# Statistics, norms, stores and an opening on TensorE: four edits to an interleaved convolution and FFN kernel

## The chip, the cores and the metric

The kernel runs on one core of a Trainium2 chip, in a single launch. The metric is the time of one execution on the device, in microseconds (us). A smaller number is better.

## What is computed

The reference holds two layers that share their weights. Each adds a gated long convolution and then a GELU-gated FFN to a residual stream x of 2048 tokens by 576 features, which starts as `A_q`. Cut to what matters:

```python
x = x + A(layernorm(x), k, v, shift_k, ssm_k, ssm_D)   # A(q, ...) = q * y
x = x + B(layernorm(x), w_gate, w_up, w_down)
x = x + A(layernorm(x), k, v, shift_k, ssm_k, ssm_D)
x = x + B(layernorm(x), w_gate, w_up, w_down)

kv = (4-tap causal convolution of k with shift_k, per feature) * v
y  = irfft(rfft(kv, padded to 4096) * rfft(ssm_k, padded))[:2048] + kv * ssm_D
B(x) = (gelu_tanh(x @ w_gate) * (x @ w_up)) @ w_down      # 576 -> 4608 -> 576
layernorm(x) = (x - mean) / sqrt(var + 1e-5)              # over the 576 features
```

The inputs and the output are bf16. The convolution's result y depends on k, v and the kernels only, so it is the same in both layers. A gate step is x + (x − mean) · rstd · y, row by row.

## The kernel before

*Tiling.* The tokens are cut into 4 blocks of 512, each of which is 4 tiles of 128 rows (tile j of a block holds every fourth row). The 576 features are handled as two halves of 288 columns. The convolution goes block against block in the frequency domain: the forward transforms, the sums over pairs of blocks and the inverse transforms are matrix products with tables of sines (`G`, `F1`, `F2`), which ScalarE makes at the start. Transformed kernel blocks (`Hd`) and kv blocks (`Kd`) are written to HBM and read back when a later block needs them.

*The FFN* goes in 24 visits. A visit takes one block of one layer (a unit) through one of 3 phases of 12 column tiles: 12 groups of 18 gate and up products (`gu`, L1078), a GELU on ScalarE (L1082), a product on VectorE (L1083), and 96 down products in four tiles j (`dn`, L1093). Units of the same pass share the weights of a phase; the passes are block 0 of layer 0 alone, then pairs, then the last block of layer 1 alone. Weights are loaded by SyncE (SP), into three `wgu` and three `wd` buffers.

*Before visit 0* the order is written out by hand in `begin` (L472 to L673), and each engine works through its own part of that order: the taps of the shift convolution by products of `ones` with the taps (`taps`, L521), the transposes of the first kernel block (L544), the forward products of kernel blocks 0 to 3 (`h_tile`, L563, 16 products by `G`, each half copied by ScalarE at L186), block 0's kv products on VectorE, its forward transforms, products and inverse (`inv0`, L621). Then follow the four gate steps of block 0 (`gate0`), the normalised rows (`norm0`), their transposes by TensorE into `xnT` (`turn0`), and between these the last `h_tile`s and the first products for kv block 1.

*Row statistics* come in two ways. `stat_steps` (L752) takes them on VectorE (`bn_stats` at L759, in two halves, `bn_aggr`, and an add), with the power −0.5 on GpSimd (POOL). `mean_after` (L803) and `square_task` (L810) take the row sum from an operation that accumulates it: POOL makes the negative mean `nm` (L806), ScalarE squares with `nm` as its bias and accumulates (L814), and POOL makes `ve` (L821) and `rstd` (L822). Before, the raw rows of block 0 (`x0_stats`, two calls of two tiles each, L596 and L646) and its gated rows use the first way; all later blocks use the second.

*After the start* a planner emits the other work between the products. It keeps modelled times for TensorE, VectorE and ScalarE and takes the head of a queue when its inputs should be ready: `vq` for residual and norm steps (`prep`, L870; `run_vq`, L917), `aq` for squares, `conv.spills` for what POOL does (spills, stores, `nm`, `rstd`), `conv.V`, `conv.Pq` and `conv.L` for the convolution. A step's place in the program is thereby fixed when the kernel is built. Normalised rows of later blocks are transposed by DMA on SP (`spread`, L903, two transposes per tile). `spreads` issues them, and while a norm is close `weights` (L952) holds back weight loads, which use the same queue. The rows of one tile, from its sum to its transposed rows, are: residual `mul` and `add` (L835, L847), `nm`, square, `rstd`, norm (L874), transposes.

*PSUM* is drawn from two pools: `psp` with 3 buffers, `cpsp` with 1. At the start `ps()` (L108) takes every fourth tile from `cpsp`:

```python
self.nps += 1
if self.startup and self.nps % 4:
    return self.psp.tile([P, 2, 512], F32, tag="pr", name="ps")
return self.cpsp.tile([P, 2, 512], F32, tag="cps", name="cps")
```

*The end.* In the last phase of a layer 1 unit each down tile j is summed with x into an output buffer `ob` (two buffers, L1103), and `conv.store` (L1106, issued at L266) has POOL store it to the output, 16 such stores in all. The program closes at L1164, where every DMA queue is drained.

Of the kernel before, what the change touches and what calls it, by code (L numbers as in the profile page):

```python
# [54 lines left out]
class Conv:  # L55
# [416 lines left out]
    def begin(self, gate0, turn0, x0_stats, more, scratch, wide, stay):  # L472

        tc, nc, D = self.tc, self.nc, self.D
        with ExitStack() as es:
# [44 lines left out]
            jg.append(None)  # L520
            def taps(j):  # L521
                ps = self.ps()
                for h in range(2):
                    nc.tensor.matmul(ps[:, h, 0:HW], lhsT=ones[:], rhs=sk1[:, h * HW:(h + 1) * HW, j], start=True, stop=True)
                nc.scalar.copy(out=self.halves(self.skc[:, j, :]), in_=ps[:, :, 0:HW])
# [70 lines left out]
            x0_stats(0)  # L596
            kc, A = {}, {}
# [48 lines left out]
            x0_stats(1)  # L646
# [3 lines left out]
            more(2)  # L650
            gate0(0)
# [25 lines left out]
def ssm_geglu_kernel(ctx, tc, A_q, A_k, A_v, A_shift_k, A_ssm_k, A_ssm_D, B_x, B_w_gate, B_w_up,  # L677
# [92 lines left out]
    def gate_steps(c, j, v, second):  # L770
        def mul():
            xa = (x_c if second else x_b)[c][:, j, :]
            if second:
                v["t"] = gwork.tile([P, D], F32, tag="g_t", name="g_t")[:]
            else:
                if j == 0:
                    x_c[c] = xpool.tile([P, RT, D], F32, name=f"x_c{c}", tag="x")
                v["t"] = x_c[c][:, j, :]
            nc.vector.scalar_tensor_tensor(out=v["t"], in0=xa, scalar=v["mv"][:, 0:1],
                                           in1=conv.y[c][:, j, :], op0=ALU.subtract, op1=ALU.mult)  # L780
            if second and j == RT - 1:
                conv.y_used[c] = t.dve + 1.0

        def add():
            xa = (x_c if second else x_b)[c][:, j, :]
            nc.vector.scalar_tensor_tensor(out=x_c[c][:, j, :], in0=v["t"], scalar=v["rstd"][:, 0:1], in1=xa,  # L786
                                           op0=ALU.mult, op1=ALU.add)
        return [(("y", c, j), C_ST, mul), (0.0, C_ST, add)]
# [66 lines left out]
    gvars = {}  # L855

# [13 lines left out]
    def prep(ui, j):  # L870
# [46 lines left out]
    def run_vq(limit):  # L917
# [11 lines left out]
        else:  # L929
            r = NEVER if len(xn_made) >= 2 else need[1].get("rstd_at", NEVER)  # L930
# [46 lines left out]
    with tc.manual_schedule():  # L977
        make_identity(nc, ident[:])
        g0 = early_stats(0)
        vs0 = [{} for _ in range(RT)]  # L980
    
        def norm0(j):
            xn = xnp.tile([P, XW], BF16, tag="xn", name="xn")
            v = vs0[j]
            nc.vector.tensor_scalar(out=xn[:, 0:D], in0=x_c[0][:, j, :], scalar1=v["mv"][:, 0:1],
                                    scalar2=v["rstd"][:, 0:1], op0=ALU.subtract, op1=ALU.mult)
# [3 lines left out]
        def turn0(j):  # L990
# [4 lines left out]
            for b in range(NKC):  # L995
                c0 = b * P if b < 5 else HK + (b - 5) * P
                nc.tensor.transpose(pt[:, b // 5, (b % 5) * P:(b % 5 + 1) * P], xn0[j][:, c0:c0 + P], ident[:])
            nc.scalar.copy(out=xnT_of[0][:, 0:5, tok], in_=pt[:, 0, 0:5 * P].rearrange("p (b q) -> p b q", q=P))
            nc.vector.tensor_copy(out=xnT_of[0][:, 5:NKC, tok], in_=pt[:, 1, 0:4 * P].rearrange("p (b q) -> p b q", q=P))
# [169 lines left out]
```

## Time and profile before

| what | us |
|---|---|
| median of 3 runs | 979.71 (978.53 to 980.3) |
| the profiled execution's own time | 979.42 |
| its span in the profile | 977.7 |
| TensorE (PE) busy | 947.3, 97% of the span |
| VectorE (DVE) busy | 542.1, 55% |
| ScalarE (ACT) busy | 301.9, 31% |
| GpSimd (POOL) busy | 139.9, 14% |
| gate and up products, L1078, 5184 of them | 568.8 |
| down products, L1093, 2304 of them | 296.7 |

How to read the profile's lines: a group's line has the line of the code, the engine, the operation, what it writes and reads with the shapes, the count after an x, then the busy time and the mean of one in ns, then the idle time of the engine just before them and what ended most of it. In a view in order of time the first column is the start in us from the span's start, the second the length; a bracket holds the wait before it and what ended that wait. `PEld` is TensorE's weight load, which overlaps its products. SPq and POOLq are the instruction sequences of SP and POOL with their DMA issues. A line such as "x3: 46/108/9861" gives the least, median and longest duration in ns of three such entries, and then the time from the first to the last.

### The profile page before, as it was taken

Reading aid. Unit: us, or ns where it says so; the run is one execution under the profiler, and the core shown is the slowest. Engines: PE = TensorE matmul, PEld = TensorE weight load, DVE = VectorE, ACT = ScalarE, POOL = GpSimd, SP = SyncE. Lnnn points to the kernel's source line nnn. Section 1 sums busy time; section 2 is a strip of 40 time slices with the busy share of each in tenths; the row PEclk is TensorE's granted clock in tenths of the full one; section 3 lists DMA queues with packets and bytes.
Section 4 is the critical chain, followed back from the end, with each engine's and each line's share of the span. In section 5 each row is a group of like instructions: output and inputs, shape, how many; then the busy total and the mean of one; then the engine's idle time right before and its main releaser. Section 6 shows DMA issues by size and latency. Waiting matters only on the chain.

```text
span 977.7 us, 19269 instructions
## 1 busy us (share of the span) xinstructions
PE 947.3 (97%) x8240; PEld 547.4 (56%) x8240; DVE 542.1 (55%) x986; ACT 301.9 (31%) x549; POOL 139.9 (14%) x299
## 2 busy tenths in 40 slices
PE   7979999899999999999999999999999999999995
PEld 4755554536556466465565565466456556556543
DVE  8878887867687476887323333663333335433331
ACT  7845213432222522413212411342211213221120
POOL 2343100521101112412000100130000002100000
PEclk9999999989999999999999999999999999999998
DMA  7989975964952551497360360293540630596710
GB/s 181 309 236 288 263 162 141 203 154 102 234 157 74 113 156 36 92 225 141 71 152 1 72 148 13 50 186 94 99 120 2 126 93 8 108 245 151 146 38 24
DMA packets 128538, 127.48 MB, mean 130 GB/s; under 512 B 45571, under 2 KB 121028, under 8 KB 128452
## 3 DMA queue, kind: packets, MB, share of 16 engines
q1 hardware_dynamic: 119184, 90.26, 43.3%
q0 software_dynamic: 9136, 35.08, 11.2%
q8 instruction: 64, 1.05, 0.5%
q10 hardware_dynamic: 132, 0.91, 0.3%
q14 instruction: 22, 0.18, 0.1%
HBM read 105.58 MB, written 10.62 MB: 119 GB/s over the span
## 4 chain that ended last, share of the span: by engine, by line
PE 80%; issue 13%; DVE 4%; ACT 1%; DMA 1%; POOL 0%; POOLq 0%; SPq 0%; DVEq 0%
PE gu L1078 50%; PE dn L1093 24%; PE cps L232 2%; PE cps L258 1%; PE cps L205 1%; PE ps L184 1%; DMA xnT<-xn 1%; DVE stats L759 0%; POOL out_dram L266 0%; DVE yb L226 0%; DVE prod L222 0%; DVE prod L225 0%; DVE yb L617 0%; DVE kvt L160 0%; DVE x_c L786 0%
## 5 line engine op out<-in xcount | busy, mean ns | idle before, releaser
L1078 PE MATMUL gu<-xnT,wgu 64*128 64x512 bf16 x5184 | 568.8, 377 | 6.7 <-DMA xnT<-xn 3.7
L1078 PEld LDWEIGHTS <-wgu 64*128 64x128 bf16 x5184 | 252.5, 94 | 313.4 <-issue 15.5
L1083 DVE TENSOR_TENSOR hT<-ga,gu 128x512 bf16<-128x512 f32 x288 | 197.9, 687 | 277.3 <-ACT ga L1082 276.2
L1082 ACT ACTIVATE ga<-gu 128x512 f32<-128x512 f32 x288 | 172.0, 597 | 547.4 <-PE gu L1078 546.1
L1093 PE MATMUL dn<-wd,hT 128*128 128x288 bf16 x2304 | 296.7, 286 | 0.0
L1093 PEld LDWEIGHTS <-hT 128*128 128x128 bf16 x2304 | 223.6, 98 | 65.1 <-issue 9.3
L1114 DVE TENSOR_TENSOR x_c<-x_c,dn 128x576 f32<-128x576 f32 x64 | 48.2, 753 | 88.1 <-PE dn L1093 87.8
L806 POOL TENSOR_SCALAR nm<-s 128x1 f32<-128x1 f32 x56 | 18.7, 336 | 372.1 <-DVE x_c L1109 157.8
L814 ACT ACTIVATE junk<-x_c,nm 128x576 bf16<-128x576 f32 x44 | 33.8, 769 | 23.6 <-POOL nm L806 23.6
L266 POOL DMA_DIRECT2D out_dram<-ob x16 | 8.8, 553 | 185.0 <-DVE ob L1103 185.0
L822 POOL TENSOR_TENSOR rstd<-ve,neghalf_t 128x1 f32<-128x1 f32 x56 | 34.6, 617 | 4.7
L226 DVE TENSOR_TENSOR sum<-prod 128x576 bf16<-128x576 bf16 x72 | 33.0, 458 | 3.0
L184 PEld LDWEIGHTS <-G 128*128 128x128 bf16 x256 | 25.6, 101 | 10.6 <-DVE h L546 2.1
L184 PE MATMUL ps<-h,G 128*128 128x288 bf16 x192 | 27.3, 299 | 3.0 <-DVE h L546 1.9
L1103 DVE TENSOR_TENSOR ob<-x_c,dn 128x576 bf16<-128x576 f32 x16 | 12.1, 754 | 31.6 <-PE dn L1093 21.8
L324 POOL DMA_DIRECT2D hr<-Hd x32 | 17.6, 549 | 63.7 <-DVE prod L225 63.5
L316 POOL DMA_DIRECT2D kr<-Kd x24 | 13.4, 560 | 91.6 <-DVE prod L225 91.6
L821 POOL TENSOR_SCALAR ve<-ss 128x1 f32<-128x1 f32 x56 | 16.4, 293 | 60.3 <-ACT junk L814 60.2
L232 PE MATMUL cps<-sum,ident 128*128 128x288 bf16 x144 | 24.9, 287 | 0.0
L160 DVE TENSOR_TENSOR kvt<-k,skc 128x1152 bf16<-128x1152 bf16 x32 | 23.7, 754 | 1.5 <-DMA k<-in_A_k_dram 1.0
L208 ACT COPY eo<-cps 128x576 f32<-128x576 f32 x24 | 15.3, 636 | 15.9 <-PE cps L205 11.1
L213 DVE TENSOR_TENSOR kc<-eo 128x288 bf16<-128x288 f32 x48 | 19.3, 453 | 1.5 <-ACT eo L208 1.5
(111 smaller groups left out, 472.7 us busy)
## 6 DMA issues: line engine op xcount, KB each, us to landing
wgu<-in_B_w_gate_dram SPq DMA_DIRECT2D x45, 576.0 KB, 5.8
wd<-in_B_w_down_dram SPq DMA_DIRECT2D x30, 864.0 KB, 7.0
wgu<-in_B_w_up_dram SPq DMA_DIRECT2D x45, 512.0 KB, 7.8
hr<-Hd POOLq DMA_DIRECT2D x32, 288.0 KB, 4.7
kr<-Kd POOLq DMA_DIRECT2D x24, 288.0 KB, 4.7
Hd<-h POOLq DMA_DIRECT2D x12, 288.0 KB, 4.2
Kd<-kc POOLq DMA_DIRECT2D x12, 288.0 KB, 7.7
k<-in_A_k_dram POOLq DMA_DIRECT2D x3, 1008.0 KB, 11.6
```

What stands on the lines that cost most here:

```text
L160: nc.vector.tensor_tensor(out=st[dst][:], in0=self.kt_[b][:, s0:s0 + 2, :], in1=self.skc[:, j, :].unsqueeze(1).to_broadcast([P, 2, D]), op ...
L184: nc.tensor.matmul(ps[:, h, 0:HW], lhsT=G[:, i, s * NFQ + kt * P: s * NFQ + (kt + 1) * P], rhs=src[:, i, h * HW:(h + 1) * HW], start=(i == ...
L213: self.nc.vector.tensor_tensor(out=dst, in0=eo[:, 0, :], in1=eo[:, 1, :], op=op)
L226: nc.vector.tensor_tensor(out=dst, in0=pr[:, 0, :], in1=pr[:, 1, :], op=ALU.subtract if part == 0 else ALU.add)
L232: nc.tensor.matmul(ps[:, h, 0:HW], lhsT=self.ident[:], rhs=pr[:, h * HW:(h + 1) * HW], start=first, stop=last)
L814: nc.scalar.activation(out=junk[:], in_=get_x(), func=ACT.Square, bias=v["nm"][:, 0:1], accum_out=v["ss"][:])
L822: nc.gpsimd.tensor_tensor(out=v["rstd"][:], in0=ve[:], in1=neghalf_t[:, 0:1], op=ALU.pow)
L1078: nc.tensor.matmul(pair[:, s, :], lhsT=w[r0:r0 + HK, k, gi * P:(gi + 1) * P], rhs=xnT[r0:r0 + HK, b, :], start=(k == 0), stop=(k == NKC - 1))
L1082: nc.scalar.activation(out=ga[:], in_=pair[:, 0, :], func=ACT.Gelu_apprx_tanh)
L1083: nc.vector.tensor_tensor(out=hT[:, fi, :], in0=ga[:], in1=pair[:, 1, :], op=ALU.mult)
L1093: nc.tensor.matmul(acc[:, h, 0:HW], lhsT=hT[:, fi, j * P:(j + 1) * P], rhs=d[:, fi % WT, h * HW:(h + 1) * HW], start=(fi == 0), stop=(fi = ...
L1114: nc.vector.tensor_tensor(out=xh, in0=xh, in1=acc[:, :, 0:HW], op=ALU.add)
```

## The change

Four things are changed.

1. *Block 0's statistics.* The gate's `add` accumulates the row sum, and `mean_after` and `square_task` follow it, in place of `stat_steps` on the gated rows; `gate0` pops `nm`, square and `rstd` from their queues at once. The raw rows of tiles 2 and 3 get their statistics right behind those of tiles 0 and 1. The gate order is 0, 2, 1, 3; `norm0` and `turn0` follow two tiles behind their gates; in the first two turns ScalarE makes both copies to `xnT`. The last `h_tile` stands behind the last turn, and eight instead of four kv products of block 1 are issued before visit 0.
2. *Norms of later blocks.* In layer 0 the norm of a tile is queued two tiles behind its residual step instead of one, and three instead of two normalised tiles may wait for their transposes.
3. *The last visit's stores* are issued by SP, and the last tile is computed half by half, each half with its own output buffer and store.
4. *The opening.* One more PSUM tile is drawn at the start, and 16 products of `ones` with `ones` (128 columns each) write to it. Nothing reads them.

The diff, cut to its core:

```diff
+            ps = self.ps()
+            for _ in range(16):
+                nc.tensor.matmul(ps[:, 0, 0:P], lhsT=ones[:], rhs=ones[:], start=True, stop=True)
+
             def taps(j):
...
             x0_stats(0)
+            x0_stats(1)
             kc, A = {}, {}
...
             pair0(1, 1)
-            x0_stats(1)
             inv0(1)
             inv0(3)
...
+            self.kv1 = self.kv_ops(1)
+            ops = iter(self.kv1)
...
             gate0(0)
+            gate0(2)
             h_tile(2, 2, self.hrp)
-            gate0(2)
             h_tile(2, 1, self.hrp)
+            gate0(1)
+            norm0(0)
             h_tile(2, 3, self.hrp)
-            turn0(0)
-            gate0(1)
+            turn0(0, True)
+            gate0(3)
+            norm0(2)
             h_tile(3, 0, self.hrp)
-            turn0(2)
-            self.kv1 = self.kv_ops(1)
+            turn0(2, True)
+            norm0(1)
+            kv1_ops(2)
+            h_tile(3, 2, self.hrp)
+            norm0(3)
+            turn0(1, False)
+            kv1_ops(2)
             h_tile(3, 1, self.hrp)
-            gate0(3)
-            h_tile(3, 2, self.hrp)
-            turn0(1)
-            for need, op in self.kv1[:2]:
-                op()
+            turn0(3, False)
+            kv1_ops(4)
             h_tile(3, 3, self.hrp)
-            turn0(3)
-            for need, op in self.kv1[2:4]:
-                op()
...
+            v["s"] = small.tile([P, 1], F32, tag="s", name="s")
+            nc.vector.scalar_tensor_tensor(out=x_c[c][:, j, :], in0=x_c[c][:, j, :], scalar=g["rstd"][:, 0:1],
+                                           in1=x_b[c][:, j, :], op0=ALU.mult, op1=ALU.add, accum_out=v["s"][:])
+            mean_after(v, 0.0)
+            square_task(lambda: x_c[c][:, j, :], v)
...
-        if j > 0:
-            tasks.append(norm(j - 1))
+        lag = 2 if layer == 0 else 1
+        if j >= lag:
+            tasks.append(norm(j - lag))
         if j == RT - 1:
-            tasks.append(norm(j))
+            tasks += [norm(i) for i in range(RT - lag, RT)]
...
-            r = NEVER if len(xn_made) >= 2 else need[1].get("rstd_at", NEVER)
+            r = NEVER if len(xn_made) >= 3 else need[1].get("rstd_at", NEVER)
...
+            (nc.scalar.copy if act else nc.vector.tensor_copy)(
+                out=xnT_of[0][:, 5:NKC, tok], in_=pt[:, 1, 0:4 * P].rearrange("p (b q) -> p b q", q=P))
             nc.scalar.copy(out=xnT_of[0][:, 0:5, tok], in_=pt[:, 0, 0:5 * P].rearrange("p (b q) -> p b q", q=P))
-            nc.vector.tensor_copy(out=xnT_of[0][:, 5:NKC, tok], in_=pt[:, 1, 0:4 * P].rearrange("p (b q) -> p b q", q=P))
...
-            for _, _, run in gate_steps(0, j, gvars[0][j], False) + stat_steps(0, j, "l_", vs0[j]):
+            for _, _, run in gate_steps(0, j, gvars[0][j], vs0[j]):
                 run()
-            if seen0:
-                norm0(seen0[-1])
-            seen0.append(j)
-            if len(seen0) == RT:
-                norm0(j)
+            conv.spills.pop()[1]()
+            aq.pop()[2]()
+            conv.spills.pop()[1]()
...
-        conv.step(1, kv=conv.kv1[4:], loaded=True)
+        conv.step(1, kv=conv.kv1[8:], loaded=True)
...
+                if wb == NWB - 1 and j == RT - 1:
+                    dst = out2[c * CH:(c + 1) * CH, :].rearrange("(p j) d -> p j d", j=RT)[:, j, :]
+                    for h in range(2):
+                        for fi in range(FP):
+                            down(fi, h)
+                        ob = work.tile([P, D], BF16, tag="ob", name="ob")
+                        nc.vector.tensor_tensor(out=ob[:, 0:HW], in0=xh[:, h, :], in1=acc[:, h, 0:HW], op=ALU.add)
+                        nc.sync.dma_start(out=dst[:, h * HW:(h + 1) * HW], in_=ob[:, 0:HW])
+                    break
...
-                    conv.store(out2[c * CH:(c + 1) * CH, :].rearrange("(p j) d -> p j d", j=RT)[:, j, :], ob,
-                               t.pe + 0.2 + C_EVD + LAG)
+                    dst = out2[c * CH:(c + 1) * CH, :].rearrange("(p j) d -> p j d", j=RT)[:, j, :]
+                    if wb == NWB - 1:
+                        nc.sync.dma_start(out=dst, in_=ob[:])
+                    else:
+                        conv.store(dst, ob, t.pe + 0.2 + C_EVD + LAG)
```

More of the change, by code (lines that the diff above doesn't have):

```diff
@@ L768, in stat_steps, with gate_steps, early_stats @@
         return [(("xb", c) if pfx == "e_" else 0.0, C_BN, lambda: half(0)), (0.0, C_BN + 0.25, lambda: (half(1), aggr()))]
-    def gate_steps(c, j, v, second):
+    def gate_steps(c, j, g, v):
         def mul():
[L772 to L779, printed above, removed]
+            if c not in x_c:
+                x_c[c] = xpool.tile([P, RT, D], F32, name=f"x_c{c}", tag="x")
+            nc.vector.scalar_tensor_tensor(out=x_c[c][:, j, :], in0=x_b[c][:, j, :], scalar=g["mv"][:, 0:1],
                                            in1=conv.y[c][:, j, :], op0=ALU.subtract, op1=ALU.mult)
-            if second and j == RT - 1:
-                conv.y_used[c] = t.dve + 1.0
         def add():
[L785 to L788, printed above, removed]
+            v["s"] = small.tile([P, 1], F32, tag="s", name="s")
[3 more added lines that the diff above has]
+            square_task(lambda: x_c[c][:, j, :], v)
+        return [(0.0, C_ST, mul), (0.0, C_ST, add)]
+    gvars = {}
+    def early_stats(c):
+        gvars[c] = [{} for _ in range(RT)]
+        return [s for j in range(RT) for s in stat_steps(c, j, "e_", gvars[c][j])]
     aq = deque()
@@ L979, in ssm_geglu_kernel @@
         g0 = early_stats(0)
-        vs0 = [{} for _ in range(RT)]
+        vs0 = [{"pfx": "l_"} for _ in range(RT)]
         def norm0(j):
@@ L1023, in more @@
                 load_x(1)
-        conv.begin(gate0, turn0, lambda k: [run() for _, _, run in g0[4 * k:4 * k + 4]], more,
+        conv.begin(gate0, norm0, turn0, lambda k: [run() for _, _, run in g0[4 * k:4 * k + 4]], more,
                    lambda dt: xtp.tile([P, RT if dt == I32 else 2, D], dt, tag="xnT", name="ang"),
```

26 lines of the change are left out of this document (14 added, 12 removed).

## The prediction

> **What bounds the kernel now.** I read the busy table by stretches first, then the waits of PE, then the order of time at the four places where PE stands. Columns of the first view: stretch, length, busy time and count of PE, weight loads, DVE, ACT, POOL, then clock, DMA share, GB/s.
>
> ```profile
> 42.30:66.10 23.80, 18.30 (x166) 14.30 (x165) 18.97 (x47) 14.74 (x23) 10.00 (x15) 1.00 0.85 231
> 66.10:191.20 125.10, 125.03 (x1066) 70.82 (x1065) 105.63 (x199) 47.09 (x90) 30.53 (x59) 1.00 0.86 219
> 191.20:197.40 6.20, 0.47 (x5) 0.17 (x6) 1.40 (x4) 0.00 (x0) 1.57 (x5) 0.82 0.82 183
> 197.40:966.00 768.60, 768.42 (x6756) 436.56 (x6756) 378.18 (x661) 206.22 (x382) 83.97 (x191) 1.00 0.48 108
> 966.00:977.70 11.70, 0.00 (x0) 0.00 (x0) 0.73 (x1) 0.00 (x0) 0.54 (x1) 0.67 0.04 13
> ```
>
> From 66.1 on PE is full (125.03 of 125.10, 768.42 of 768.60) except at one seam, 191.2 to 197.4, and in the last 11.7 us. The change adds no product there, so only three stretches can give: the front (before 66.1), the seam (at most 6.2 us), the tail (at most 11.7). Of PE's waits in the front the longest in total is (us in total, times, longest):
>
> ```profile
> PE xps L997 <- DVE xn L985: 3.9, 2, 2.7
> ```
>
> PE waits there for block 0's normalised rows, which DVE makes.
>
> **The tail: the last visit's stores on SP, the last one in halves.**
>
> ```profile
> 954.00 11.93 PE L1093 MATMUL dn<-wd,hT 128*128 128x288 bf16 x96
> 965.97 0.76 DVE L1103 TENSOR_TENSOR ob<-x_c,dn 128x576 bf16<-128x576 f32 x1 [2.19 <-PE dn L1093]
> 967.02 0.54 POOL L266 DMA_DIRECT2D out_dram<-ob  x1 [2.40 <-DVE ob L1103]
> DMA to landing us min/median/max: 2.0/2.0/2.0
> L1164 SPq DRAIN  x3: 7/7/7, 969.3 to 977.1; - x3
> L1164 POOLq DRAIN  x3: 46/108/9861, 967.0 to 977.4; - x3
> ```
>
> PE ends at 965.93 (954.00 + 11.93). The store, issued by POOL at 967.02, has landed 2.0 later, at 969.0, and SP drains at 969.3. But POOL's first DRAIN, right behind its last DMA, starts at 967.0 and takes 9.861 us: to 976.9. The program ends 0.8 later, at 977.7. So neither the data nor SP ends the kernel; POOL's drain does, 7.6 us after SP. With the change POOL's last DMA is a store of the visit before (near 864), its drain stands 100 us ahead of the end, and its 9.9 us hide behind the last visit's products.
>
> What is left after PE's end: the wait of DVE (0.04), the half-width sum, SP's pick-up (0.05, an estimate), the landing, SP's 0.3 from landing to drain, and the closing 0.8. For the half sum the row of the same width is
>
> ```profile
> L213 DVE TENSOR_TENSOR kc<-eo 128x288 bf16<-128x288 f32 x48 | 19.3, 453 | 1.5 <-ACT eo L208 1.5
> ```
>
> 0.45. For a landing of an SP store in a quiet chip no row exists; the nearest is POOL's 2.0, the same bytes at the same place, which I take. Sum 0.04 + 0.45 + 0.05 + 2.0 + 0.3 + 0.8 = 3.65 against 977.7 − 965.93 = 11.77: **8.1 off**. Bounds: SP's own DMAs land in 2.5, 3.2 or 9.2 (least, median, most; the row stands with the rivals). With 3.2 the second `ob` buffer comes in too: the last half takes the tile of j = 2, written until 2.14 before PE's end (2.94 per j − 0.04 − 0.76) and free 3.2 + 0.05 later, at +1.1; then 1.1 + 0.45 + 0.05 + 3.2 + 1.1 = 5.9, 5.9 off. Above, nothing is left to gain but the 2.0. I take **8.0, from 5.5 to 8.3**.
>
> The Trainium skill speaks against this: "DMA: Bandwidth & Descriptors", section "Issuing engines are not separate DMA queues", says that the issuing engine only changes the sequencer's issue time. By that alone the move is worth POOL's 0.54 at most; it is the first rival. The same page's table "SWDGE vs HWDGE vs iDMA" gives first bytes at about 0.6 us from SP against 1 us from POOL; by it the sum would be 0.4 better. No run shows either yet.
>
> **The front: row statistics.** Rows of before, in order of time, then groups (busy, mean ns):
>
> ```profile
> 29.18 0.76 DVE L222 TENSOR_TENSOR prod<-kc,h 128x1152 bf16<-128x1152 bf16 x1 [1.69 <-ACT kc L197]
> 42.34 0.81 DVE L759 BATCH_NORM_STATS2 stats<-x_b 128x6 f32<-128x288 bf16 x2
> 44.19 1.14 PE L184 MATMUL ps<-h,G 128*128 128x288 bf16 x8
> 44.78 0.81 DVE L779 SCALAR_TENSOR_TENSOR x_c<-x_b,mv,y 128x576 f32<-128x576 bf16 x1
> 45.05 1.28 ACT L649 ACT_TABLE_LOAD   x1
> 46.46 0.63 ACT L186 ACTIVATE h<-ps 128x576 bf16<-128x576 f32 x1
> 46.55 0.82 DVE L759 BATCH_NORM_STATS2 stats<-x_c 128x6 f32<-128x288 f32 x2
> 57.48 0.98 PE ps L184 x8
> 62.14 0.68 PE L997 MATMUL xps<-ident,xn 128*128 128x128 bf16 x9 [0.74 <-ACT h L186]
> 66.10 17.90 PE L1078 MATMUL gu<-xnT,wgu 64*128 64x512 bf16 x162 [0.82 <-ACT xnT L998]
> L186 ACT ACTIVATE h<-ps 128x576 bf16<-128x576 f32 x10 | 6.4, 649 | 5.3 <-DMA Hd<-h 3.5 <-PE ps L184 1.7
> L998 ACT COPY xnT<-xps 128x640 bf16<-128x640 bf16 x4 | 2.8, 690 | 2.0 <-PE xps L997 2.0
> L806 POOL TENSOR_SCALAR nm<-s 128x1 f32<-128x1 f32 x56 | 18.7, 336 | 372.1 <-DVE x_c L1109 157.8
> L814 ACT ACTIVATE junk<-x_c,nm 128x576 bf16<-128x576 f32 x44 | 33.8, 769 | 23.6 <-POOL nm L806 23.6
> L822 POOL TENSOR_TENSOR rstd<-ve,neghalf_t 128x1 f32<-128x1 f32 x56 | 34.6, 617 | 4.7
> L821 POOL TENSOR_SCALAR ve<-ss 128x1 f32<-128x1 f32 x56 | 16.4, 293 | 60.3 <-ACT junk L814 60.2
> ```
>
> *Moved:* the raw rows' statistics of tiles 2 and 3, 42.34 to 44.78 = 2.44, go ahead of the product at 29.18, where DVE waits 1.69. DVE's work from there on is 2.44 − 1.69 = 0.75 later, and dense, so the first gate product starts at 42.34 + 0.75 = 43.1 instead of 44.78. The inverse products' copies and the table load behind them are 0.75 later too.
>
> *Removed:* four tiles' DVE statistics of x_c, 0.82 for the two halves alone (46.55), so 3.3 and more in all. *Added* per tile: nm 0.34 on POOL, a square 0.77 on ACT, ve 0.29 and rstd 0.62 on POOL, 2.0, and four crossings at 0.1 (an estimate): 2.4 from sum to rstd. The accumulated sum itself costs DVE nothing that I count: under 0.1 per tile.
>
> *The new wait.* ACT and POOL work in order. Tile 0's sum is done at 43.1 + 1.8 = 44.9, nm at 45.3; its square waits for ACT, free after the table load at 46.46 + 0.75 + 0.1 = 47.3, and ends at 48.1; rstd 49.2. Tile 2's sum is done at 46.7, but its nm stands on POOL behind tile 0's rstd: 49.6, its square 49.7 to 50.5. Behind this square on ACT are the copies of h tiles (2,2) and (2,1), which started at 46.46 and now start at 50.5. PE starts these four halves at 44.19 + 0.75 = 44.9, has four PSUM pairs, and stops at 44.9 + 4 × 0.98 = 48.9, until the first is copied at 51.2.
>
> *From 50.5* ACT sets the pace up to the last transposed rows: 12 h copies × 0.65, two squares × 0.77, four xnT copies × 0.69 and the two of four blocks that come over from DVE (0.57 each, an estimate by 0.69 for five): 7.8 + 1.5 + 2.8 + 1.1 = 13.2, with 0.5 for waits: 64.2. PE turns tile 3 just before (62.6 to 63.2, 0.68) and computes the h tile (3,3), now behind that turn, 2 × 0.98: 65.2. Then visit 0 starts; before it did so at 66.5 (162 products × 0.1085 = 17.6, back from 84.0). **1.3 off.** Bounds: a PE without a wait from 44.9, 7 h tiles × 1.96 + 4 × 0.68 = 16.4, starts at 61.3 (5.2 off); if the squares of tiles 1 and 3 also stop ACT, 2.4 − 0.77 = 1.6 each, 1.9 is lost.
>
> *At nothing:* eight instead of four kv products (0.77 each, 3.1 more) before visit 0; they lie on DVE, which has 4.8 idle in this stretch and loses 3.3 of statistics. Uncovered, two of them ahead of tile 3's xnT copy would cost 1.5.
>
> **The opening: 16 dummy products, and one more PSUM tile drawn,** so that every later pool choice shifts by one.
>
> ```profile
> 2.69 1.69 PE L524 MATMUL ps<-sk,ones 1*128 1x288 bf16 x6 [2.69 <-DMA sk<-in_A_shift_k_dram]
> 5.61 2.88 PE L544 MATMUL hps<-ident,hn 128*128 128x128 bf16 x20 [0.72 <-ACT skc L525]
> 10.44 4.95 PE L184 MATMUL ps<-h,G 128*128 128x288 bf16 x24 [1.95 <-DVE h L546]
> 11.40 1.43 DVE L160 TENSOR_TENSOR kvt<-k,skc 128x1152 bf16<-128x1152 bf16 x2 [1.02 <-DMA k<-in_A_k_dram]
> ```
>
> PE is idle to 2.69. Sixteen at the transposes' pace (2.88 / 20 = 0.144) take 2.3 from 1.1: taps 0.7 late, the transposes up to 0.7 late; DVE has 1.02 of wait for k at 11.40 that takes this. If the clock is up sooner, the first 16 h products, some 4.0 long (later ones take 0.98 for eight), save up to 2.0 on PE, but the kv chain on DVE, which waits for k, is next. I take **0, from −0.5 to +0.7**. "TensorE: Matmul & The Clock Gate" of the Trainium skill, section "What's actually happening", wants some 3.4 us of sustained work before full speed and puts a cold 128-column product at 0.107; by it the dummies take 1.7, end as the taps' data come, and cost nothing. Sum unchanged, the +0.7 gone.
>
> **The seam: norms two tiles behind.**
>
> ```profile
> 189.67 0.57 DVE L877 TENSOR_SCALAR xn<-x_c,nm,rstd 128x576 bf16<-128x576 f32 x1
> 186.97 6.03 SPq L906 DMA_TRANSPOSE xnT<-xn  x4
> 197.36 1.89 PE L1078 MATMUL gu<-xnT,wgu 64*128 64x512 bf16 x8 [3.67 <-DMA xnT<-xn]
> ```
>
> In the planned order of after, tile 3's norm follows the third residual sum and two cross sums directly; a product (0.76, as at 29.18) and a sum (some 0.45) that stood between now come later. PE's interleaved forward products put that residual some 0.5 later. So xn, now at 189.67, is 0.7 earlier, its two transposes, and PE's start at 197.36: **0.7 off, from −1 to +4** (the norm of tile 2 moves ahead by 2, and the transposes no longer queue).
>
> **Sum.** 8.0 + 1.3 + 0 + 0.7 = 10.0. The profiled execution took 979.42, 1.7 more than its span of 977.7, and the median of the runs is 979.71: 979.4 − 10.0 = 969.4, and 969.7 by the median. I say 969.6.
>
> **Rivals.**
> 1. *The drain stays* (does not do what it says): the 9.9 us are a closing routine of POOL that waits for all engines, wherever its last DMA was. For it: all queues close with a DRAIN. Against: POOL's starts at 967.0, before SP and the landing, with no wait before it. Then 979.7 − 2.0 − 0.5 = 977.2. Chance 0.10.
> 2. *ACT becomes the bound of the front* with POOL's order in it, and the seam gives nothing: lost 1.9 there, 979.7 − 8.0 + 1.9 = 973.6. For it: ACT's 13.2 from 50.5 leave it no slack. Against: PE has 1.96 per tile to do meanwhile. Chance 0.10.
> 3. *Slower: the transposes of the last block queue behind a weight load.*
>
> ```profile
> 648.09 23.42 PE gu L1078 x216
> 632.38 0.64 SPq L733 DMA_DIRECT2D wgu<-in_B_w_gate_dram  x1
> L906 SPq DMA_TRANSPOSE xnT<-xn x40: 1199/1252/2227, 211.4 to 671.0; - x40
> DMA to landing us min/median/max: 2.5/3.2/9.2
> ```
>
> In after's SP order three weight loads stand ahead of all eight transposes of block 3; before, four went first. They start at 632.4 + 2.0 = 634.4; PE needs them at 648.1, with the next pass. At the median of 1.25 to issue and 3.2 they are there at 634.4 + 7 × 1.25 + 3.2 = 646.4. It decides from 1.5 each; at the largest values of the row, 634.4 + 7 × 2.23 + 9.2 = 659.2, PE stands 11.1: 969.6 + 11.1 = 980.7. Chance 0.04.
>
> Forecast 0.76, its own range 967.0 to 972.5. The range of all: 966.5 to 974.0, which takes in rival 2 and the bounds of tail and front. Within 0.2% (2.0 us, what a measurement can tell) lies half of rival 1, so faster 0.91, same 0.05, slower 0.04.
>
> **What would show it.** Tail: POOL's long DRAIN ends long before the last product; from PE's last product to the end 3.5 to 6 us. Front: first gu product near 65.2; a wait of the ACT square on POOL's nm near 48 to 50; PE standing near 49 to 51. Seam: PE's wait for xnT about 0.7 shorter. Wrong: a POOL DRAIN of 10 us that ends with the kernel, or a new wait of PE between 200 and 960.

## The result and the profile after

The changed kernel takes 974.18 us (median of 5 runs, 973.51 to 976.38); the kernel before took 979.47 beside it (5 runs, 978.53 to 980.3). The ratio is 0.9952, interval 0.9937 to 0.9967: faster by some 5, where 10 were forecast, and 0.2 above the range of 966.5 to 974.0. The profiled execution took 973.51 with a span of 971.7, which is 6.0 less than the 977.7 of before.

The busy table of the changed kernel, cut where PE starts visit 0, where it stops and starts at the seam, and where its last product ends (columns as in the prediction):

```profile
42.30:65.82 23.52, 19.43 (x174) 15.08 (x172) 15.28 (x31) 18.15 (x33) 10.74 (x20) 1.00 0.84 225
65.82:191.57 125.75, 125.34 (x1067) 69.47 (x1066) 100.83 (x191) 47.76 (x91) 29.56 (x60) 1.00 0.86 213
191.57:199.46 7.89, 0.01 (x1) 0.00 (x1) 0.81 (x3) 0.00 (x0) 1.29 (x4) 0.80 1.15 271
199.46:968.36 768.90, 768.32 (x6758) 436.70 (x6758) 381.41 (x666) 206.22 (x382) 83.09 (x188) 1.00 0.48 108
968.36:971.70 3.34, 0.00 (x0) 0.00 (x0) 0.45 (x1) 0.00 (x0) 0.00 (x0) 0.92 0.08 25
```

The tail shrank from 11.77 to 3.34, but PE's last product ends at 968.36, 2.4 later than before (965.93). PE's waits say where (us in total, times, longest):

```profile
PE gu L1087 <- DMA xnT<-xn: 7.9, 1, 7.9
PE dn L1103 <- DVE ob L1112: 0.5, 1, 0.5
PE cps L205 <- ACT eo L208: 0.3, 1, 0.3
```

At the seam (where PE goes from the last down product of visit 2 to the first gate product of block 1) PE now stands 7.9 in one piece. Before it was 3.7 for these rows and 2.1 just ahead of that, which the profile puts down to a step of DVE: 5.8 in all. The 0.5 is new and stands in the halved last tile.

**Tail.** The last visit in order of time, and the drains (least/median/longest in ns, first and last start):

```profile
966.22 0.45 DVE L1112 TENSOR_TENSOR ob<-x_c,dn 128x288 bf16<-128x288 f32 x1 [0.72 <-PE dn L1103]
966.73 1.63 PE L1103 MATMUL dn<-wd,hT 128*128 128x288 bf16 x12 [0.55 <-DVE ob L1112]
968.39 0.45 DVE L1112 TENSOR_TENSOR ob<-x_c,dn 128x288 bf16<-128x288 f32 x1 [1.72 <-PE dn L1103]
L1187 POOLq DRAIN  x3: 46/107/12017, 865.8 to 971.5; - x3
L1187 SPq DRAIN  x3: 7/7/7, 970.9 to 971.2; - x3
```

POOL's long drain (12.0 now) starts at 865.8 and is over 90 us ahead of the end. The bracket in the second row is the price of the halves: the second half's first product waits until DVE has read the first half.

**Front,** in order of time:

```profile
43.23 0.81 DVE L786 SCALAR_TENSOR_TENSOR x_c<-x_b,mv,y 128x576 f32<-128x576 bf16 x1
49.36 0.78 ACT L827 ACTIVATE junk<-x_c,nm 128x576 bf16<-128x576 f32 x1 [1.16 <-POOL nm L819]
50.81 1.14 PE L184 MATMUL cps<-h,G 128*128 128x288 bf16 x8 [1.65 <-ACT h L186]
63.26 0.66 PE L1009 MATMUL xps<-ident,xn 128*128 128x128 bf16 x9
65.82 6.43 PE L1087 MATMUL gu<-xnT,wgu 64*128 64x512 bf16 x58
```

These are the forecast's own steps: gate at 43.1, ACT's square behind POOL's nm, PE standing from 48.9 to about 51, tile 3's turn by 63.2, first gate product at 65.2. In the first row the gate starts at 43.23; the brackets of the second and third are ACT's wait for `nm` and PE's standing, from 49.16 to 50.81.

**Seam.** SP, DVE, POOL and PE in order of time, then the seam's later transposes (ns to issue, first and last start) with their landing, of the changed kernel:

```profile
180.78 0.62 SPq L745 DMA_DIRECT2D wgu<-in_B_w_gate_dram  x1
183.19 11.48 SPq L918 DMA_TRANSPOSE xnT<-xn  x6
189.36 0.57 DVE L888 TENSOR_SCALAR xn<-x_c,nm,rstd 128x576 bf16<-128x576 f32 x1
189.47 0.62 POOL L760 DMA_DIRECT2D x_b<-in_A_q_dram  x1
190.81 1.07 POOL L263 DMA_DIRECT2D Kd<-kc  x2 [0.72 <-DVE kc L213]
199.49 2.82 PE L1087 MATMUL gu<-xnT,wgu 64*128 64x512 bf16 x12 [7.91 <-DMA xnT<-xn]
...
L918 SPq DMA_TRANSPOSE xnT<-xn x7: 1209/1388/3052, 179.4 to 192.8; - x7
DMA to landing us min/median/max: 4.8/7.7/8.0
...
q0 software_dynamic: 609, 2.29, 35.3%
```

The last row is POOL's DMA queue from 180 to 200 (packets, MB, share). The same views of the kernel before, with its weight load and its x load:

```profile
179.87 0.62 SPq L733 DMA_DIRECT2D wgu<-in_B_w_gate_dram  x1
181.95 11.05 SPq L906 DMA_TRANSPOSE xnT<-xn  x6
191.82 0.61 POOL L748 DMA_DIRECT2D x_b<-in_A_q_dram  x1
...
L906 SPq DMA_TRANSPOSE xnT<-xn x6: 1200/1254/1336, 181.9 to 191.7; - x6
DMA to landing us min/median/max: 2.6/5.6/7.0
...
q0 software_dynamic: 304, 1.18, 18.8%
```

Tile 3's xn is 0.3 earlier (189.36 against 189.67), but its transposes are issued 1.1 later (the last at 192.8 against 191.7) and land in 7.9 and 7.1, so PE starts 2.1 later. POOL's queue moved 2.29 MB in these 20 us, where it moved 1.18 before. The weight load stands at the same place in both kernels, behind two of the eight transposes.

### The profile page after: what moved, and what is told of

Read it like the earlier page. It is cut to its first block, busy times and chain, and to the rows that moved or that the text cites. A ratio compares the mean times of both kernels' runs of the same rounds, so it can differ in the third digit from the quotient of the medians.

```text
span 971.7 us, 19304 instructions
## 1 busy us (share of the span) xinstructions
PE 949.8 (98%) x8256; PEld 547.9 (56%) x8256; DVE 537.3 (55%) x973; ACT 305.4 (31%) x559; POOL 139.5 (14%) x303
## 4 chain that ended last, share of the span: by engine, by line
PE 92%; DVE 4%; DMA 3%; ACT 1%; issue 0%; POOL 0%; ACTq 0%; SPq 0%; DVEq 0%
PE gu L1087 58%; PE dn L1103 28%; PE cps L232 2%; PE cps L258 1%; PE cps L205 1%; DMA k<-in_A_k_dram 1%; DMA xnT<-xn 1%; DMA Hd<-h 1%; DVE kvt L160 1%; PE ps L184 0%; DVE prod L225 0%; DVE yb L226 0%; DVE kvt L165 0%; PE ps L258 0%; DVE stats L771 0%
## 5 line engine op out<-in xcount | busy, mean ns | idle before, releaser
L827 ACT ACTIVATE junk<-x_c,nm 128x576 bf16<-128x576 f32 x48 | 36.9, 769 | 22.2 <-POOL nm L819 22.1
L835 POOL TENSOR_TENSOR rstd<-ve,neghalf_t 128x1 f32<-128x1 f32 x60 | 36.9, 614 | 5.0
L834 POOL TENSOR_SCALAR ve<-ss 128x1 f32<-128x1 f32 x60 | 17.7, 296 | 64.8 <-ACT junk L827 64.6
L266 POOL DMA_DIRECT2D out_dram<-ob x12 | 6.7, 561 | 88.9 <-DVE ob L1123 88.9
```

Of the source, the lines that this page charges most:

```text
L827: nc.scalar.activation(out=junk[:], in_=get_x(), func=ACT.Square, bias=v["nm"][:, 0:1], accum_out=v["ss"][:])
L835: nc.gpsimd.tensor_tensor(out=v["rstd"][:], in0=ve[:], in1=neghalf_t[:, 0:1], op=ALU.pow)
```

## The experiments

Each run was timed 4 to 11 times, with the kernel before on the same chip. The ratio is to that. "First G" is the first forward product of kernel block 0, "gate" the first gate product, "seam" PE's waits for block 1's rows, all from the profiled execution (for late_x, warm_seam and warm_more the profile names nothing that ended the seam's wait).

| run | first G | gate | seam | span | ratio (interval) |
|---|---|---|---|---|---|
| before | 10.44 | 66.10 | 5.8 | 977.7 | 1 |
| changed | 10.50 | 65.82 | 7.9 | 971.7 | 0.9952 (0.9937 to 0.9967) |
| sp_whole | 12.50 | 68.94 | 5.7 | 972.5 | 0.9920 (0.9904 to 0.9936) |
| pool_stores | 10.44 | 65.18 | 7.8 | 980.2 | 1.0017 (1.0006 to 1.0027) |
| lag_one | 10.44 | 65.92 | 6.7 | 970.3 | 0.9925 (0.9908 to 0.9942) |
| load_held | 10.44 | 65.56 | 5.8 | 970.3 | 0.9925 (0.9908 to 0.9943) |
| pe_turns | 10.69 | 65.47 | 0.9 | 963.6 | 0.9869 (0.9847 to 0.9890) |
| nm_first | 12.85 | 66.52 | 8.3 | 973.0 | 0.9946 (0.9931 to 0.9961) |
| halves_apart | 12.15 | 66.78 | 8.0 | 973.5 | 0.9931 (0.9914 to 0.9948) |
| no_dummies | 13.09 | 67.78 | 9.1 | 974.4 | 0.9948 (0.9932 to 0.9964) |
| changed_again | 10.44 | 65.53 | 9.8 | 973.5 | 0.9958 (0.9943 to 0.9973) |
| late_x | 11.09 | 66.46 | 5.2 | 969.5 | 0.9927 (0.9909 to 0.9945) |
| warm_seam | 14.11 | 69.66 | 4.1 | 977.8 | 0.9965 (0.9953 to 0.9978) |
| all_mended | 13.14 | 66.68 | 0.9 | 964.1 | 0.9860 (0.9845 to 0.9874) |
| before_lag_two | 10.43 | 67.06 | 0 | 970.6 | 0.9915 (0.9900 to 0.9930) |
| warm_more | 13.45 | 68.66 | 2.6 | 975.1 | 0.9953 (0.9939 to 0.9966) |
| held_late_x | 12.99 | 67.84 | 4.0 | 971.2 | 0.9892 (0.9876 to 0.9908) |
| planner_as_before | 10.44 | 65.53 | 0 | 961.1 | 0.9841 (0.9818 to 0.9864) |
| two_edits | 13.09 | 68.39 | 0 | 964.0 | 0.9847 (0.9826 to 0.9868) |
| all_mended_two | 13.42 | 66.82 | 0 | 961.9 | 0.9811 (0.9790 to 0.9833) |

First G moves between 10.4 and 14.1 from run to run, with and without dummies, among kernels that open alike, as the first kernel rows (`hn`) land. Each kernel but the changed one has one profiled execution, so whether it also moves between executions of one kernel is not shown; the two of the changed kernel have 10.50 and 10.44. In warm_seam, the latest, PE waits for them this long:

```profile
PE hps L548 <- DMA hn<-in_A_ssm_k_dram: 4.4, 1, 4.4
```

So a front is compared by gate minus first G. With the front of before (before, sp_whole, before_lag_two, two_edits) it is 55.3 to 56.6, in the mean 56.0; with the changed front and its dummies (twelve of the executions in the table) 54.6 to 55.6, in the mean 55.1; the ranges overlap at their ends.

**The tail.** sp_whole is the kernel before with SP's stores alone; pool_stores is the changed kernel with POOL's.

```diff
# sp_whole (on the kernel before)
-                    conv.store(out2[...], ob, t.pe + 0.2 + C_EVD + LAG)
...
+                    if wb == NWB - 1:
+                        nc.sync.dma_start(out=dst, in_=ob[:])
...
# pool_stores (on the changed kernel, both places)
-                        nc.sync.dma_start(out=dst, in_=ob[:])
+                        nc.gpsimd.dma_start(out=dst, in_=ob[:])
```

> The kernel before with one edit: the last visit's four stores are issued by SP, whole rows, no halves. If POOL's long drain starts behind POOL's last DMA, wherever that is (the theory): from the end of the products 0.04 + 0.76 for the whole sum + 0.05 + 2.0 landing + 0.3 + 0.8 = 4.0 instead of 11.8, a span near 970 and a time near 971.7, ratio 0.992. If the drain is a closing routine that waits for all engines, or the issuing engine changes only the issue time: 978.9, ratio 0.9995, and a drain of some 9.9 us at the end.

> The changed kernel with its five last stores issued by POOL again, halves kept. Theory (the drain follows POOL's last DMA): from the end of the products 0.5 to the last store, then 9.9 of drain and 0.8: 11.2 instead of 3.3, so 7.9 slower than the changed kernel, 982. Rival (the issuing engine changes only the issue time): 0.5 slower, 974.7.

The drains of POOL in sp_whole, then in pool_stores:

```profile
L1167 POOLq DRAIN  x3: 46/99/12363, 866.8 to 972.2; - x3
```

```profile
L1187 POOLq DRAIN  x3: 46/99/9941, 969.5 to 979.9; - x3
```

The long drain follows POOL's last DMA, wherever that is, and is hidden if that is early. In sp_whole PE ends at 956.66 + 11.93 = 968.59 and the span at 972.5: 3.9 for the whole-row store. The halves leave 3.34 and cost 0.55 of waiting: 3.9 too. They give nothing.

```diff
# halves_apart
                     for h in range(2):
+                        if h:
+                            acc = cpsp.tile([P, 2, 512], F32, tag="cps", name="dn")
```

> The changed kernel with a PSUM tile of its own for the second half of the last tile. Theory (the second half's first product waits until DVE has read the first half, since both lie in one tile): PE's wait of 0.55 on the output sum is gone, from the start of the last visit's down products to PE's end 12.0 instead of 12.64, time 0.55 less, 973.6. Rival (it waits for something else): unchanged, 974.2.

The wait is gone: in the profile all 96 down products stand as one row, of 11.93. The time hardly moved, as in the profiled execution its first G was 1.65 later; its ratio's interval overlaps the changed kernel's, so the 0.5 is seen in the trace and not in the time.

**The opening and the front.** no_dummies takes the 16 products and the extra PSUM tile away; nm_first changes the order:

```diff
             gate0(0)
             gate0(2)
+            stat0()        # square, ve, rstd of the oldest tile
             h_tile(2, 2, self.hrp)
+            stat0()
             h_tile(2, 1, self.hrp)
...
-            turn0(0, True)
+            turn0(0, False)
...
```

> The changed kernel without the 16 dummy products and without the extra PSUM tile. Theory (they change nothing that counts: the kv chain on DVE starts when k is there, at 11.4 to 11.7): first h product at 10.4 to 10.5, first gate product within 0.4 of 65.8, time 974.2, within 0.05% of the changed kernel. Rival (a clock that is up sooner gains on the h products): their first 16 take 0.6 or more longer than 4.0, and the time is 1 longer, 975.

> The changed kernel with another order in the start: the negative means of tiles 0 and 2 both stand on POOL ahead of the first rstd, the square of tile 2 stands on ACT behind two copies of an h tile, and DVE makes the four-block copies of all four turns. Theory F (POOL's order and ACT set the pace from 48 to 64): ACT no longer waits 1.16 for nm, starts its copies at 48.2 instead of 50.1, and has 1.2 less to do: first gate product at 63.5 to 64.5 instead of 65.8, time 972.5. Rival G (PE, DVE or the spills of h hold it): 65.3 or later, 974.

Without dummies gate minus first G is 54.7, among the 54.6 to 55.6 with them, and the products by G start as late as `hn` lets them. In the changed kernel the dummies lie between 1.09 and the taps' first product at 2.77:

```profile
1.09 1.88 PE L523 MATMUL ps<-ones 1*128 1x128 bf16 x16 [1.09 <-DVE pis L507]
10.50 4.02 PE L184 MATMUL ps<-h,G 128*128 128x288 bf16 x16 [1.21 <-DVE h L550]
```

The taps start 0.08 later than before (2.69), and the first 16 products by G still take 4.02, where those of before took 3.98. Nothing shows a gain or a loss of the dummies. nm_first has 53.7, and the two kernels below that share its order 53.5 and 53.4, 1.6 less than the mean of 55.1: POOL's order and ACT were a part of the front's pace, as rival 2 of the prediction has it. In nm_first's profiled execution a first G 2.3 later hides this, and its ratio is the changed kernel's within the interval: a gain in time is not shown.

**The seam.** lag_one puts the lag back to one; load_held and late_x move a transfer out of the transposes' way; held_late_x moves both; pe_turns does without them for two tiles.

```diff
# lag_one
-        lag = 2 if layer == 0 else 1
+        lag = 1
...
-            r = NEVER if len(xn_made) >= 3 else need[1].get("rstd_at", NEVER)
+            r = NEVER if len(xn_made) >= 2 else need[1].get("rstd_at", NEVER)
# load_held: no weight load from the last down products of visit 2 to visit 3
-        while due:
+        while due and not seam[0]:
...
# late_x
-        at_start = {..., (1, 0): [("x", 2)], ...
+        at_start = {..., (2, 0): [("x", 2)], ...
# pe_turns: in spreads()
+            if ui == 1 and j >= RT - 2:
...
+                    nc.tensor.transpose(pt[:, b // 5, (b % 5) * P:(b % 5 + 1) * P], xn[:, c0:c0 + P], ident[:])
```

> The changed kernel with the norms of later blocks one tile behind again; all else as changed. Theory A (the order of the norms is what made the wait at the seam longer): the wait of PE for transposed rows near 191 to 199 falls from 7.9 to 5 to 6, time near 972, ratio 0.9925. Rival B (the wait comes from what else moved: weights 0.9 later, the other start): it stays at 7 to 8, time near 974, ratio 0.995.

> The changed kernel in which the weight load of 1.15 MB that stands among the seam's transposes on SP (issued at 180.8) goes behind all eight of them. Theory C (the transposes share the DMA queues with this load, are issued late and land late): they land in 2.5 to 5 instead of 4.8 to 8.0, and PE's wait falls from 7.9 to 3 to 5: time 970 to 971.5, ratio 0.991. Rival D (POOL's two Kd writes and the x load at 189.5 to 191.9 do it): the last two still land in 7 or more, PE's wait stays at 7 or more, 974, ratio 0.995.

> The changed kernel with the load of x for block 2 (576 KB, issued by POOL at 189.5, ahead of the last two transposes) one visit later. Theory D2 (it takes part in delaying the last transposes): they land in 5 to 6.5 instead of 7.1 and 7.9, PE's wait falls from 7.9 to about 6.3, time 1.5 less. Rival (the weight load alone does it): wait 7.7 to 8.0, same time.

> The changed kernel with both transfers out of the seam: the weight load behind the transposes and the load of x one visit later. Theory (what is in flight beside them sets when the transposes land, and both add up): PE's wait 7.9 - 2.1 - 2.7 = 3.1, and with so little idle time the clock falls less; ratio 0.9905. Rival (they overlap, or the transposes' own pace of 1.25 and 2.5 sets it): 4.5 to 5.5, ratio 0.992.

> The changed kernel, but at the seam tiles 2 and 3 of the normalised rows are transposed by PE (9 products each, copies by ACT and DVE as in the start), behind the last down product, not by DMA. Theory E (the wait at the seam is the way of the last rows through SP and the DMA queues, from xn at 189.4 to 199.5): PE's wait of 7.9 falls to 1.5 to 2.5, with 1.3 more of products: 4 to 5 off, 969 to 970, ratio 0.990. Rival (tile 1's transposes, which land near 192.5, or the copies hold PE next): a wait of 4 or more is left, 972, ratio 0.993.

> The changed kernel itself, beside the three that follow and the kernel before on the same chip. By its first runs: ratio 0.995, PE's wait at the seam 7.8 to 8.0, the start of the first product by G between 10.4 and 13.1 as the first kernel rows land.

lag_one waits 6.7, 4.4 for the rows and 2.3 for a cross sum, between its two theories; the pair was badly put, as before_lag_two shows below. Held, the weight load takes 2.1 off the wait, the load of x 2.7, both together 3.9. The wait is no constant, though: changed_again has 9.8 with the same order, and the six executions that share the changed kernel's seam (changed, pool_stores, halves_apart, nm_first, no_dummies, changed_again) have 7.8 to 9.8. The 5.8, 5.2 and 4.0 lie below all six, so either transfer counts; how much each is worth, and whether they share a part, is not settled by one execution each. With PE's turns it is 0.9, and the time falls by more than the wait: 8.1 of span. With 1.2 of products added and a gate product 0.3 earlier, some 2 are left over, and they are PE's clock. The stretches from 196 on, of the changed kernel (the column behind POOL's is the granted clock):

```profile
196.00:198.00 2.00, 0.00 (x0) 0.00 (x0) 0.00 (x0) 0.00 (x0) 0.00 (x0) 0.59 0.95 256
200.00:202.00 2.00, 2.00 (x12) 0.71 (x12) 0.00 (x0) 0.00 (x0) 0.00 (x0) 0.50 1.09 358
204.00:206.00 2.00, 2.00 (x22) 0.90 (x20) 1.78 (x4) 0.66 (x3) 0.21 (x1) 1.00 0.13 37
```

At half the clock 12 gate products fall into 2 us, where 22 do later. The kernel before loses its clock at the seam too:

```profile
200.00:202.00 2.00, 2.00 (x14) 0.65 (x12) 0.32 (x1) 0.60 (x1) 0.00 (x0) 0.51 0.96 314
```

Two runs fill the wait with products that nothing reads:

```diff
+            if wb == NP and first:
+                wp = psp.tile([P, 2, 512], F32, tag="pr", name="warm")
+                for _ in range(80):          # 130 in warm_more
+                    nc.tensor.matmul(wp[:, 0, 0:P], lhsT=ident[:], rhs=ident[:], start=True, stop=True)
```

> The changed kernel with 80 products of the identity by itself between the last down product before the seam and the first gate product behind it; nothing reads them; 80 x 0.074 = 5.9 of PE's wait of 7.9. Theory W (an idle PE loses its clock, 0.50 in the rows from 196 on, and gets it back 4 behind its restart, which costs 2): the granted clock stays at 1.00, the first 100 gate products take 10.9 instead of 12.8, time 2 less, ratio 0.993. Rival (the clock falls with something else, such as the load of the DMA queues): 0.50 all the same, no gain.

> As the run with 80 products of the identity, with 130 of them: 130 x 0.058 = 7.5 of the wait, so that at most 2.5 of idle time is left. Theory W (the clock falls after some 3 to 5 of idle time and comes back about 4 behind the restart): 1.00 throughout, the first 100 gate products take 10.9 instead of 12.8, ratio 0.994 where the changed kernel has 0.9955. Rival: 0.50 behind the restart again, no gain.

With 80, PE still stood 4.1, restarted at 0.50 and had its clock back only 5.9 later. With 130 it stood 2.6, and the clock stayed (the row of warm_more that holds the restart):

```profile
204.00:206.00 2.00, 1.64 (x14) 0.72 (x16) 0.00 (x0) 0.00 (x0) 0.00 (x0) 1.00 1.08 340
```

In both the rows themselves came later: from the last down product to the gate products some 8.8 and 10.1 instead of 7.9. So it is shown that the clock falls with PE's idle time, but no gain in time from these products.

**What made the seam worse.** before_lag_two is the kernel before with the norms two behind alone.

> The kernel before with the norms of later blocks two tiles behind, and nothing else of the change. Theory N (the order of the norms alone makes the wait longer): PE's waits from 191 to 200, 3.7 + 2.1 before, become 7.5 to 9 in one, and the time is 1.5 to 3 longer, ratio 1.002. Rival (it takes the other edits, such as the eight kv products, to make the transfers meet): 5 to 6 as before, ratio 0.9995 to 1.0005.

Both theories fell: it gains, 0.85%, and PE does not wait at all from 100 to 960. Its clock stays at 1.00 from 190 to 215, and planner_as_before's does too. Its seam, in order of time:

```profile
178.24 10.44 SPq L907 DMA_TRANSPOSE xnT<-xn  x8
178.93 0.82 DVE L849 SCALAR_TENSOR_TENSOR x_c<-x_c,rstd,x_b 128x576 f32<-128x576 f32 x1
185.02 0.57 DVE L877 TENSOR_SCALAR xn<-x_c,nm,rstd 128x576 bf16<-128x576 f32 x1
188.78 0.62 SPq L733 DMA_DIRECT2D wgu<-in_B_w_gate_dram  x1
191.63 23.48 PE L1079 MATMUL gu<-xnT,wgu 64*128 64x512 bf16 x216
```

And the changed kernel at the same place:

```profile
178.02 0.81 DVE L855 SCALAR_TENSOR_TENSOR x_c<-x_b,nm,y 128x576 f32<-128x576 bf16 x1
178.75 0.82 DVE L213 TENSOR_TENSOR kc<-eo 128x288 bf16<-128x288 f32 x2
181.64 0.81 DVE L862 SCALAR_TENSOR_TENSOR x_c<-x_c,rstd,x_b 128x576 f32<-128x576 f32 x1
```

Tile 3's residual sum stands at 178.93 in the one and at 181.64 in the other, behind cross sums and a down sum. With it, its xn comes at 185.02 or at 189.36. And the weight load stands behind all eight transposes or among them. In the kernel before it stands among them too (179.87, behind the first two): the norms two behind take it away, and the change's other edits put it back. `weights` holds loads back only while a norm heads the planner's queue or rows wait for their transposes. That the late sum headed it in the changed kernel is read from this code and the order, not measured. With the load out of the way, the transposes of before_lag_two land in 2.5 to 2.7.

The planner's start differs in two ways: the four squares of `begin` move its modelled ScalarE time, and eight kv products are done instead of four. With one of these put back, the order of instructions still has the load among the transposes; with both, it stands behind them. That kernel, and two more:

```diff
# planner_as_before (on the changed kernel)
-            kv1_ops(4)
+            kv1_ops(2)       # and the two behind turn0(1) go
...
+        t.act = 0.0
         hpool = pool("hT", 1)
...
-        conv.step(1, kv=conv.kv1[8:], loaded=True)
+        conv.step(1, kv=conv.kv1[4:], loaded=True)
# two_edits: before_lag_two with the stores of sp_whole
# all_mended_two: planner_as_before with nm_first and halves_apart
```

> The changed kernel, but the planner starts as in the kernel before: four kv products before visit 0 instead of eight, and its modelled ScalarE time set to 0 behind the start (the four squares that the change puts there had moved it). By the order of instructions all eight transposes of the seam then stand ahead of the weight load, as in before_lag_two. Theory P (the seam was lost by where the planner put tile 3's residual step and the load, not by the norms two behind): no wait for transposed rows from 100 to 960, the clock at 1.00, 7.9 + 2 less than the changed kernel: 964.5, ratio 0.9855. Rival (the two orders differ, but the start's other changes bring a wait of 3 or more back): 968 or more, ratio 0.989.

> The kernel before with two edits of the change: norms two tiles behind, and the last visit's stores by SP in whole rows. Theory (they add up: 8.7 and 7.8 measured alone): 981 - 16.5 = 964.5, ratio 0.983. Rival (they share a part): 968, ratio 0.987.

> The kernel of planner_as_before with the means first in the start and a PSUM tile of its own for the second half of the last tile: 1.3 + 0.5 below it, 962.7, ratio 0.9835. Rival (by then the opening's first rows set the end of the start): as planner_as_before.

> Three edits of the runs before together on the changed kernel: PE transposes tiles 2 and 3 at the seam, the means stand first in the start, the second half of the last tile has its own PSUM tile. By their traces 8.1 + 1.3 + 0.5 below the changed kernel, whose ratio is 0.995: ratio 0.985, 966 where the kernel before takes 981.

all_mended (pe_turns, nm_first and halves_apart on the changed kernel) came to 0.9860. No wait for transposed rows is left in the other three. planner_as_before, 0.9841, has the changed kernel's edits but for those counts; it shows what the whole change would have given without the planner's turn. Two edits alone give 0.9847, within its interval. all_mended_two has the lowest ratio: 0.9811, 962.7 (median of 4 runs, 960.55 to 963.66) where the kernel before takes 980.39.

## Why the prediction was wrong, point by point

- *Tail, 8.0 forecast.* Right. 11.77 behind PE's end became 3.34, 8.4 less, and 0.55 of that was given back in PE: 7.9. The step that costed the halves at nothing left out that two halves in one PSUM tile make PE wait for DVE. The landing of 2.0 taken for SP's store was 1.6 for the halves, so 3.34 was left and not 3.65.
- *Rival 1, the drain stays:* ruled out by pool_stores and sp_whole. By the Trainium skill's "Issuing engines are not separate DMA queues" ("DMA: Bandwidth & Descriptors") the move was worth the issue time alone; the 7.8 (0.80%) by which sp_whole beats before say otherwise, and the measurement decides. The first-byte figures that the prediction takes from the same page of the Trainium skill stand in its section "Specifications", not in the table it names; the trace has the same sign and less: SP's whole-row stores landed in 1.7 to 1.8, POOL's in 2.0.
- *Front, 1.3 forecast.* Right in its mechanism, and too large. Each step came within 0.7 of its time, and gate minus first G fell by 0.9 in the mean (56.0 to 55.1). In the profiled pair the gate product is only 0.3 earlier (66.10 to 65.82), and some 0.1 come behind it, where the first 162, without the sums between them, took 17.8 before and 17.7 now.
- *Rival 2, 973.6,* lies nearest to the measured time, but not by its mechanism: the front gained, and the loss is the seam's.
- *Opening, 0 forecast.* Nothing measured speaks against it. The dummies took 1.9 by their row, and not the sum's 2.3. What the prediction had not seen is that the first rows' landing differs by up to 3.7 between the profiled executions, of which the prediction had one.
- *Seam, 0.7 of gain forecast, from −1 to +4.* This is the step that failed: "So xn, now at 189.67, is 0.7 earlier, its two transposes, and PE's start at 197.36". xn was 0.3 earlier, but the step let the transposes keep the issue and landing times that they had before. In the new order the x load went out 2.3 earlier, two more writes of Kd went out, two block reads (`kr`, `hr`) were issued at 178.3 and 178.9, where the last one of before was at 176.4, and tile 2's norm came 1.7 earlier (186.16 to 184.44), so that its transposes stood closer behind the weight load: the first took 3.05 to issue and landed in 7.6, where before it took 1.25 and 4.4. PE started 10.1 behind the start of tile 3's norm (189.36 to 199.46) and not 7.7 (189.67 to 197.36). Lost: 2.1, where 0.7 was to be gained. The bound "the transposes no longer queue" was the wrong way round. Which of these transfers took how much of the 2.1 stays open; that the order of instructions decides is shown by planner_as_before, which has the change's edits but for the start's counts, another order and no wait.
- *What was overlooked altogether* is that this edit, left alone, is worth some 8, 5.8 of wait and about 2 of clock (the kernel before restarted at 197.36 and ran at half its clock until 202.0); the interval of the seam stopped at 4, since the prediction took the order of instructions as given and did not ask which part of it the norms had caused.
- *Rival 3, a load ahead of block 3's transposes:* did not come; PE waits for nothing between the seam and the last tile.

In sum: 7.9 of the tail and some 0.4 of the front, less 2.1 at the seam and 0.3 for `eo` ahead of it, make 5.9 of the 6.0 by which the span fell. Against the forecast of 10.0 the seam is 2.8 short, the front 0.9, `eo` 0.3 and the tail 0.1.

## What to carry to other kernels

An edit to the start of a kernel whose order comes from a planner moves decisions a hundred us later: compare the order of instructions at every place where PE already waits, edit by edit, before a gain is booked. Where a few transposes end a wait, list every other transfer in flight beside them, and price their landing by the crowd, not by the row of before. And look at which queue issues the last DMA: here hiding its closing drain was worth 7.8 of a time that fell by 5.3 in all.

## What the runs showed of the hardware

- POOL's drain behind its last DMA took 9.9 to 12.4 us in four kernels, though the last store of before had landed 2.0 behind its issue, and also where it lay over 90 us ahead of the end (12.0 in the changed kernel). SP's drains took 7 ns each.
- An idle PE lost half its clock 2.2 to 5.2 us behind its last product where the wait had no product in it (4.8 in the changed kernel, 3.2 in warm_seam, 2.2 in nm_first, 5.2 in no_dummies), and got it back 3.0 to 5.9 behind its restart (3.7 in the changed kernel, 4.6 in before, 5.9 in warm_seam), which cost half of that. The stretch at half the clock lasted 6.8 in eight executions, 10.2 in four (changed_again is one) and 3.4 in late_x: whole multiples of 3.4. In warm_more 2.6 of idle time kept the clock, which is one execution, and the 2.2 of nm_first says that it need not. "TensorE: Matmul & The Clock Gate" of the Trainium skill, section "What's actually happening", gives about 3.4 us for either turn, in windows that run freely. The lengths of the stretches agree with it; the 2.2 of nm_first is shorter than one such window, and there the measurement decides. The prediction had used this page for the opening alone.
- Transposes by DMA that land in 2.5 to 2.7 where the weight load stands behind them (before_lag_two) took 4.8 to 8.0 in the changed kernel, beside 1.15 MB of weights and the 2.29 MB of POOL's queue, and up to 12.1 in another execution of the same kernel (tile view of changed_again); their issue on SP went from 1.25 to as much as 3.05.
